# Modulation sums over partitions, moved from matmuls on TensorE to all-reduces on GpSimd

## The chip, the core and the metric

The kernel runs on one core of a Trainium2 chip. The metric is the device time of one execution in microseconds (us), the median of several. The core's engines are named as the profile names them: PE (TensorE), DVE (VectorE), ACT (ScalarE), POOL (GpSimd) and SP (SyncE, which only issues DMAs here).

## The reference, cut

One transformer block over x (1 x 2048 x 512) with adaptive layer norms: six modulation vectors of 512 numbers come from c and w_mod, and shift, scale and gate the two halves of the block.

```python
mod = (_silu(c) @ w_mod).reshape(c.shape[0], 6, 1, -1)
sa, ca, ga, sb, cb, gb = (mod[:, 0], mod[:, 1], mod[:, 2], mod[:, 3], mod[:, 4], mod[:, 5])
h = _layernorm(x, axis=-1) * (1 + ca) + sa
x = x + ga * _A_ref(h, A_wqkv, A_wo)              # linear attention, 32 heads of 16
h = _layernorm(x, axis=-1) * (1 + cb) + sb
x = x + gb * _B_ref(h, B_w_gate, B_w_up, B_w_down)  # (h w_gate * h w_up) w_down
```

All is float32.

## The kernel before, in words

x has 16 tiles of 128 tokens by 512, in 4 chunks of 4. Each float32 operand of a large product is split into a high part (an fp32r rounding, by ACT) and a low part (the difference, by DVE), and a product is three matmuls: high by high, high by low, low by high. Each engine works its own queue in the order in which the code issues it (the schedule is manual: no planner moves anything), and waits on semaphores where it uses what another engine made. Tiles of 128x512 come from one pool of 99 buffers, taken in turn, so a new tile may also wait for the last reader of the buffer's old one.

The first stage makes the modulation vectors sa and ca (v=0 and 1) and K of the first chunk. Then comes the **T loop** (L646 to L695): in step i it issues the K projection of tile i+2 (`proj`, 12 matmuls of 128x512, lines L219 to L221; past the last tile a Q projection), the split of the normalized tile i+1 (`k_split_x`: xh on ACT, xl on DVE at L207) and of phi(K) of tile i+1 (`k_split`: kh on ACT at L363, kl on DVE at L364), in the first two steps of a chunk two transposed columns of the next chunk's norm and their modulation (`modulated`: f on ACT, the high part h as a cast on DVE at L304, the low part at L307), phi of tile i+2 (`k_phi`: two activations, then DVE at L331), the sum z of phi (`z_add`, L357), and `t_tile(i)`, 12 matmuls into four PSUM banks (L372 to L374). In the step before the last, zacc is split, and in the last step two matmuls with a matrix of ones (`over_rows`, L195) sum it over the partitions: zps, from which ACT makes zb. Behind the loop den0 (L706) and the tiles tt (L782 to L787) are made from zb on DVE and ACT, and PE multiplies them (L795).

Into steps 4 to 15 the table `extra` puts work for later, at the end of each step. Part of it are the other four modulation vectors, v = 2 (ga), 3 (sb), 4 (cb) and 5 (gb). For each, `mod_load` issues four DMAs of 128x512 from w_mod, and `mod_part` adds up, on DVE, the four tiles times the four columns of silu(c), into one tile acc of 128x512 (L178 for k=0, L180 for k=1 to 3). What is left is the sum of acc over its 128 partitions. For ga and gb, which are needed as a row repeated on every partition, acc is split (one ACT and one DVE instruction) and `mod_row` multiplies a matrix of ones by both parts on PE (L195) and copies the result from PSUM by ACT (L201). For sb and cb, which are needed as columns (128x4), `mod_col` multiplies each quarter of acc by a vector of ones (L185, a float32 matmul of two passes), and `col_out` adds 0 or 1 on DVE (L190). All four are used only behind the loop: ga at L770, cb and sb at L925, gb at L1280. wo's loads and splits stand in the same table.

Of the kernel before, what the change touches and what calls it, by code (L numbers as in the profile page):

```python
# [7 lines left out]

F32 = mybir.dt.float32
# [1 line left out]
AF = mybir.ActivationFunctionType  # L11
ALU = mybir.AluOpType
AX = mybir.AxisListType

P = 128
# [7 lines left out]
def tile_adaln_block(  # L23
# [12 lines left out]
    nc = tc.nc  # L36
# [3 lines left out]
    KD = D // P  # L40
# [12 lines left out]
    wo_v = wo.rearrange("(k p) n -> k p n", p=P)  # L53
# [20 lines left out]
    def B(tag, shape=(P, D), dt=F32):  # L74

        return T(tiles, tag, shape, dt)
# [32 lines left out]
    def load(src, tag, by=None):  # L109
        raw = B(tag, (P, *src.shape[1:]))[:src.shape[0]]  # L110
        (by or nc.sync).dma_start(raw, src)
        return raw
# [27 lines left out]
    raw_v = load_qkv(2)  # L140
# [38 lines left out]
            else:  # L179
                nc.vector.scalar_tensor_tensor(acc, raws[k], sc[:, k:k + 1], acc, op0=ALU.mult, op1=ALU.add)  # L180

    def mod_col(acc, ps):

        for b in range(KD):
            nc.tensor.matmul(ps[:, b:b + 1], acc[:, b * P:(b + 1) * P], ones, start=True, stop=True)  # L185
        return ps

    def col_out(v, ps, add):
        t = consts.tile([P, KD], F32, name=f"col{v}")
        nc.vector.tensor_scalar(t, ps[:, :KD], add, None, op0=ALU.add)  # L190
        return t

    def over_rows(ps, pair):
        for m, x in enumerate(pair):
            nc.tensor.matmul(ps, ones_r, x, start=m == 0, stop=m == 1)  # L195

    def mod_row(v, pair):
        ps = bank()
        over_rows(ps, pair)
        t = consts.tile([P, D], F32, name=f"row{v}")  # L200
        nc.scalar.activation(t, ps, AF.Copy)  # L201
        return t


# [110 lines left out]
    wk, wq, wv = [], [], []  # L315
# [262 lines left out]
    def mod_load(*vs):  # L578
        raw_m.update({v: load_mod(v) for v in vs})

    def mod_part(v, *ks):
        if 0 in ks:
            accs[v] = B("f")
        mod_acc(accs[v], raw_m[v], ks)

    extra = {4: lambda: (wv.extend(split_raw(r) for r in raw_v[0:1]),),
             5: lambda: (wv.extend(split_raw(r) for r in raw_v[1:2]),),
             6: lambda: (wv.extend(split_raw(r) for r in raw_v[2:3]), mod_load(2),),
             7: lambda: (wv.extend(split_raw(r) for r in raw_v[3:4]),),
             8: lambda: (mod_part(2, 0, 1), mod_load(3)),  # L590
             9: lambda: (mod_part(2, 2, 3), mod_load(4)),
             10: lambda: (accs.update({2: split_raw(accs[2])}), mod_part(3, 0, 1, 2), mod_load(5)),
             11: lambda: (mod_part(3, 3), mod_part(4, 0, 1), rows.update({2: mod_row(2, accs[2])})),
             12: lambda: (raw_o.extend(load(wo_v[k], "raw") for k in range(KD)), mod_part(4, 2, 3), mod_part(5, 0), cols.update({3: col_out(3, mod_col(accs[3], bank()), 0.0)})),
             13: lambda: (mod_part(5, 1, 2, 3), wo_s.extend(split_raw(x) for x in raw_o[:1]), accs.update({5: split_raw(accs[5])}), cols.update({4: col_out(4, mod_col(accs[4], bank()), 1.0)})),
             14: lambda: (wo_s.extend(split_raw(x) for x in raw_o[1:]),), 15: lambda: rows.update({5: mod_row(5, accs[5])})}
    q_at = {4: 3}
    ahead = {}

# [1004 lines left out]
```

## Time and profile before

| | us |
|---|---|
| runs before | 553.54, 553.78, 557.78 (median 553.78) |
| profiled execution, first to last instruction | 552.4 |
| T loop, proj(6) to t_tile(15) on PE | 52.3 to 127.0 |
| PE busy | 545.8 |
| DVE busy | 432.2 |
| ACT busy | 299.5 |
| POOL busy | 176.8 |

The profiled execution's own time is told only as its span, from the first to the last instruction; the runs' times also hold what lies around it, so the median of the runs is 1.4 us above the span. In rows of the timeline the first number is the start in us from the span's start, the second the time until the end, then engine, line, operation, output and inputs, shape and count; in brackets the idle time of the engine before it and what ended that. Matmul rows overlap: the time from one start to the next is what a matmul costs PE (0.23 us for 128x512), the duration is what it takes to come through.

### The profile page before, as it was taken

How to read it: one execution, taken by the hardware profiler on the slowest of the kernel's cores; microseconds unless marked ns; L12 is line 12 of the kernel's file. 1: busy time of each engine (PE TensorE's matmuls, PEld its weight loads, DVE VectorE, ACT ScalarE, POOL GpSimd, SP SyncE). 2: the span in 40 equal slices, each digit the busy share in tenths (PEclk: the TensorE clock that was granted, in tenths of full speed). 3: DMA queues.
4: the chain of work that ended last, by engine and by line, in shares of the span. 5: the costliest groups of instructions: out<-in, count | busy, mean ns of one | idle time of the engine just before them, and what ended most of it. 6: DMA issues, size and time to landing. Idle time of an engine off the chain costs nothing. (4 is left out here: it accounts for less than half of the span.)

```text
span 552.4 us, 8146 instructions
## 1 busy us (share of the span) xinstructions
PE 545.8 (99%) x2775; PEld 460.1 (83%) x2775; DVE 432.2 (78%) x794; ACT 299.5 (54%) x535; POOL 176.8 (32%) x180
## 2 busy tenths in 40 slices
PE   8999999999999999999999999999999999999997
PEld 6888888888888888888888888878888888888886
DVE  6878779978998998865655767797577877879696
ACT  4876857456467876654545355463243534453540
POOL 2000000003527646353556644540002524242400
PEclk9999999999999999999999999999999999999999
DMA  8910224203230045195888634289786534342004
GB/s 256 373 57 1 76 77 152 77 0 77 78 115 2 0 154 189 39 316 180 285 286 274 222 123 163 87 312 391 231 259 218 173 131 138 129 146 86 1 0 153
DMA packets 58512, 83.24 MB, mean 151 GB/s; under 512 B 6564, under 2 KB 23720, under 8 KB 58472
## 3 DMA queue, kind: packets, MB, share of 16 engines
q1 hardware_dynamic: 56544, 81.16, 44.1%
q10 hardware_dynamic: 1928, 1.58, 0.9%
q8 instruction: 22, 0.36, 0.3%
q14 instruction: 18, 0.15, 0.1%
HBM read 53.02 MB, written 29.69 MB: 150 GB/s over the span
## 5 line engine op out<-in xcount | busy, mean ns | idle before, releaser
L1057 PE MATMUL bank<-h,w 128*128 128x512 f32 (+1 forms) x924 | 221.6, 391 | 0.2 <-POOL w L1020 0.2
L1057 PEld LDWEIGHTS bank<-h,w 128*128 128x128 f32 (+1 forms) x924 | 168.2, 186 | 36.2 <-POOL w L1020 0.6
L1063 ACT ACTIVATE bank<-bank 128x512 f32<-128x512 f32 (+2 forms) x46 | 26.2, 571 | 122.7 <-PE bank L1057 122.5
L1253 DVE TENSOR_TENSOR x<-acc,x 128x256 f32<-128x256 f32 x132 | 48.0, 414 | 13.7 <-PE acc L1226 13.1
L1226 PE MATMUL acc<-w,kh 128*128 128x256 f32 x308 | 57.1, 282 | 0.0
L1226 PEld LDWEIGHTS acc<-w,kh 128*128 128x128 f32 x308 | 50.6, 190 | 3.7
L1020 POOL TENSOR_TENSOR w<-raw,w 128x256 fp32r<-128x256 f32 (+3 forms) x22 | 24.7, 1121 | 73.7 <-ACT w L1013 64.1
L219 PE MATMUL bank<-w,h 128*128 128x512 f32 x112 | 44.1, 394 | 0.0
L221 PE MATMUL bank<-w,h 128*128 128x512 f32 x112 | 43.7, 390 | 0.0
L220 PE MATMUL bank<-w,h 128*128 128x512 f32 x112 | 43.6, 390 | 0.0
L1226 PE MATMUL acc<-w,kl 128*128 128x256 f32 x154 | 43.5, 283 | 0.0
L871 PE MATMUL acc<-w,xh 128*128 128x512 f32 x128 | 40.7, 399 | 0.0
L712 POOL TENSOR_TENSOR f<-h,zb 128x512 f32<-128x512 f32 x12 | 17.5, 1468 | 62.9 <-ACT zb L692 48.9
L262 POOL TENSOR_TENSOR rstd<-ve,half 128x4 f32<-128x4 f32 (+3 forms) x12 | 11.2, 935 | 81.4 <-DVE ve L259 68.0
L1083 DVE TENSOR_TENSOR phi<-bank,g 128x512 f32<-128x512 f32 (+1 forms) x22 | 15.1, 687 | 25.2 <-PE bank L1057 25.2
L1063 ACT ACTIVATE u<-bank 128x512 f32<-128x512 f32 (+1 forms) x44 | 26.1, 594 | 15.4 <-PE bank L1057 15.2
L1113 DVE TENSOR_TENSOR g<-bank,u 128x512 f32<-128x512 f32 (+1 forms) x22 | 15.2, 689 | 21.2 <-ACT u L1063 19.9
L1020 POOL TENSOR_TENSOR w<-t,w 128x512 fp32r<-128x512 f32 (+1 forms) x22 | 29.6, 1346 | 0.0
L1146 PE MATMUL acc<-w,kh 128*128 128x512 f32 (+1 forms) x76 | 29.6, 390 | 0.0
L1147 PE MATMUL acc<-w,kh 128*128 128x512 f32 (+1 forms) x76 | 29.6, 390 | 0.0
L1148 PE MATMUL acc<-w,kl 128*128 128x512 f32 (+1 forms) x76 | 29.6, 389 | 0.0
L277 ACT ACTIVATE n<-x,nmr,rstd 128x512 f32<-128x512 f32 x31 | 23.6, 808 | 10.9 <-DVE nmr L267 10.7
(204 smaller groups left out, 1187.0 us busy)
## 6 DMA issues: line engine op xcount, KB each, us to landing
right<-w SPq DMA_DIRECT2D x56, 256.0 KB, 3.7
w<-right SPq DMA_DIRECT2D x56, 256.0 KB, 4.3
x<-in_A_x_dram SPq DMA_DIRECT2D x22, 256.0 KB, 5.2
raw<-in_w_mod_dram SPq DMA_DIRECT2D x22, 256.0 KB, 3.7
raw<-in_B_w_down_dram SPq DMA_DIRECT2D x18, 256.0 KB, 3.0
side_s<-h SPq DMA_DIRECT2D x16, 256.0 KB, 2.6
h<-side_s SPq DMA_DIRECT2D x16, 256.0 KB, 5.3
raw<-in_A_wqkv_dram SPq DMA_DIRECT2D x12, 256.0 KB, 6.2
```

The lines of the kernel that those rows point to most:

```text
L219: nc.tensor.matmul(ps, ah, bh, start=begin and i == 0, stop=False)
L220: nc.tensor.matmul(ps, ah, bl, start=False, stop=False)
L221: nc.tensor.matmul(ps, al, bh, start=False, stop=end and i == n - 1)
L871: nc.tensor.matmul(yps[i], x, y, start=fresh and k + n == 0, stop=k == KD - 1 and n == 2, skip_group_check=True)
L1020: sub = lambda out, x, y: (on or nc.gpsimd).tensor_tensor(out, x, f32(y), op=ALU.subtract)
L1057: mm = lambda x, y, **kw: nc.tensor.matmul(ps, x[:, k], y, skip_group_check=True, **kw)
L1063: nc.scalar.activation(out, x, AF.Copy)
L1146: nc.tensor.matmul(dn[j], hh[:n, a:b], dh[:n], start=i == 0, stop=False)
L1147: nc.tensor.matmul(dn[j], hh[:n, a:b], dl[:n], start=False, stop=False)
L1148: nc.tensor.matmul(dn[j], hl[:n, a:b], dh[:n], start=False, stop=i == n_of - 1)
L1226: mm = lambda x, y, **kw: nc.tensor.matmul(ps, x[:, a:b], y, skip_group_check=True, **kw)
L1253: nc.vector.tensor_tensor(xt[:, halves[at]], banks[b][m], xt[:, halves[at]], op=ALU.add)
```

## The change

The four sums over partitions are made by POOL: `partition_all_reduce` of acc, 128x512, whose result stands on every partition. For the rows that is the result. For the columns the reduced tile is multiplied by the identity, repeated four times (`col_diag`, on POOL), and DVE reduces each 128-wide group to one number (`col_out`: a reduction to 128x4, and for v=4 an addition of 1). The splits of acc, the matmuls, the PSUM banks and the evictions go. The loads of the four vectors move from steps 6, 8, 9 and 10 to steps 4 to 7, the sums on DVE from steps 8 to 13 to steps 6 to 11. The reductions are issued in steps 8 (row 2), 9 (column 3), 10 (column 4) and 11 (row 5, and both multiplications by the identity), `col_out` in steps 13 and 15.

```diff
+    def over_partitions(out, acc):
+        nc.gpsimd.partition_all_reduce(out, acc, channels=P, reduce_op=ReduceOp.add)
+
+    def col_total(v, acc):
+        diag[v] = B("f")
+        over_partitions(diag[v], acc)
+
+    def col_diag(v):
+        t = diag[v].rearrange("p (b i) -> p b i", i=P)
+        nc.gpsimd.tensor_tensor(t, t, ident.unsqueeze(1).to_broadcast([P, KD, P]), op=ALU.mult)
+
+    def col_out(v, add):
         t = consts.tile([P, KD], F32, name=f"col{v}")
-        nc.vector.tensor_scalar(t, ps[:, :KD], add, None, op0=ALU.add)
-        return t
+        nc.vector.reduce_sum(t, diag.pop(v).rearrange("p (b i) -> p b i", i=P), axis=AX.X)
+        if add:
+            nc.vector.tensor_scalar(t, t, add, None, op0=ALU.add)
+        cols[v] = t
...
-    def mod_row(v, pair):
-        ps = bank()
-        over_rows(ps, pair)
+    def mod_row(v, acc):
         t = consts.tile([P, D], F32, name=f"row{v}")
-        nc.scalar.activation(t, ps, AF.Copy)
+        over_partitions(t, acc)
         return t
...
-             6: lambda: (wv.extend(split_raw(r) for r in raw_v[2:3]), mod_load(2),),
-             7: lambda: (wv.extend(split_raw(r) for r in raw_v[3:4]),),
-             8: lambda: (mod_part(2, 0, 1), mod_load(3)),
-             9: lambda: (mod_part(2, 2, 3), mod_load(4)),
-             10: lambda: (accs.update({2: split_raw(accs[2])}), mod_part(3, 0, 1, 2), mod_load(5)),
-             11: lambda: (mod_part(3, 3), mod_part(4, 0, 1), rows.update({2: mod_row(2, accs[2])})),
-             12: lambda: (raw_o.extend(load(wo_v[k], "raw") for k in range(KD)), mod_part(4, 2, 3), mod_part(5, 0), cols.update({3: col_out(3, mod_col(accs[3], bank()), 0.0)})),
-             13: lambda: (mod_part(5, 1, 2, 3), wo_s.extend(split_raw(x) for x in raw_o[:1]), accs.update({5: split_raw(accs[5])}), cols.update({4: col_out(4, mod_col(accs[4], bank()), 1.0)})),
-             14: lambda: (wo_s.extend(split_raw(x) for x in raw_o[1:]),), 15: lambda: rows.update({5: mod_row(5, accs[5])})}
+             4: lambda: (wv.extend(split_raw(r) for r in raw_v[0:1]), mod_load(2)),
+             5: lambda: (wv.extend(split_raw(r) for r in raw_v[1:2]), mod_load(3)),
+             6: lambda: (wv.extend(split_raw(r) for r in raw_v[2:3]), mod_part(2, 0, 1), mod_load(4)),
+             7: lambda: (wv.extend(split_raw(r) for r in raw_v[3:4]), mod_part(2, 2, 3), mod_load(5)),
+             8: lambda: (rows.update({2: mod_row(2, accs[2])}), mod_part(3, 0, 1, 2)),
+             9: lambda: (mod_part(3, 3), mod_part(4, 0, 1), col_total(3, accs.pop(3))),
+             10: lambda: (mod_part(4, 2, 3), mod_part(5, 0), col_total(4, accs.pop(4))),
+             11: lambda: (mod_part(5, 1, 2, 3), rows.update({5: mod_row(5, accs[5])}), col_diag(3), col_diag(4)),
+             12: lambda: (raw_o.extend(load(wo_v[k], "raw") for k in range(KD)),),
+             13: lambda: (wo_s.extend(split_raw(x) for x in raw_o[:1]), col_out(3, 0.0)),
+             14: lambda: (wo_s.extend(split_raw(x) for x in raw_o[1:]),), 15: lambda: col_out(4, 1.0)}
```

In the three places below, names carry a running number that differs between the two programs, and line numbers of the changed kernel are 7 or 8 higher.

POOL's queue from the last norm of the T loop (rstd) to the first product behind the loop (L712 before, L720 now); what stands in brackets are the engines and DMA queues that a row waits for. Before:

```order
L262 TENSOR_TENSOR rstd_885<-ve_887,half 128x4 [waits DVE_49,Activation_49,Pool_49]
L712 TENSOR_TENSOR f_1422<-h_1347,zb 128x512 [waits DVE_49,Activation_49]
L712 TENSOR_TENSOR f_1424<-h_1393,zb 128x512 [waits DVE_49,PE_49]
```

And now:

```order
L269 TENSOR_TENSOR rstd_901<-ve_903,half 128x4 [waits DVE_49,Activation_49,Pool_49]
L184 ISA
L184 ISA row_1060<-f_933 128x512 [waits DVE_49]
L184 ISA f_1130<-f_1062 128x512 [waits DMAHW7_49,DVE_49,PE_49]
L184 ISA f_1174<-f_1127 128x512 [waits DMAHW6_49,DVE_49,Activation_49]
L184 ISA row_1217<-f_1172 128x512 [waits DVE_49]
L193 ISA
L193 TENSOR_TENSOR f_1130<-f_1130,ident 128x512 [waits Pool_49]
L193 TENSOR_TENSOR f_1174<-f_1174,ident 128x512 [waits Pool_49]
L720 TENSOR_TENSOR f_1405<-h_1332,zb 128x512 [waits DMAHW4_49,DVE_49,Activation_49]
```

Between the two stand the four reductions (row 2, column 3, column 4, row 5) and the two multiplications. The two ISA rows without operands switch POOL's loaded library, to the one that has the reduction and back.

DVE's queue in steps 6 and 7 of the T loop, from the low half of a V weight (w from raw) on; xl and kl are what `t_tile` of the next step uses. Before:

```order
L207 TENSOR_TENSOR w_914<-raw_147,w_913 128x512
L207 TENSOR_TENSOR xl_939<-n_697,xh_938 128x512
L364 SCALAR_TENSOR_TENSOR kl_943<-phi_891,kh_942 128x512
L331 SCALAR_TENSOR_TENSOR phi_948<-bank_925,phi_948 128x512
L357 TENSOR_TENSOR z_176<-z_176,phi_891 128x512
L207 TENSOR_TENSOR w_968<-raw_149,w_967 128x512
L207 TENSOR_TENSOR xl_985<-n_699,xh_984 128x512
```

And now:

```order
L214 TENSOR_TENSOR w_930<-raw_147,w_929 128x512
L179 TENSOR_SCALAR f_933<-raw_787,sc 128x512
L181 SCALAR_TENSOR_TENSOR f_933<-raw_789,sc,f_933 128x512
L214 TENSOR_TENSOR xl_958<-n_697,xh_957 128x512
L371 SCALAR_TENSOR_TENSOR kl_962<-phi_907,kh_961 128x512
L338 SCALAR_TENSOR_TENSOR phi_967<-bank_944,phi_967 128x512
L364 TENSOR_TENSOR z_176<-z_176,phi_907 128x512
L214 TENSOR_TENSOR w_987<-raw_149,w_986 128x512
L181 SCALAR_TENSOR_TENSOR f_933<-raw_791,sc,f_933 128x512
L181 SCALAR_TENSOR_TENSOR f_933<-raw_793,sc,f_933 128x512
L214 TENSOR_TENSOR xl_1014<-n_699,xh_1013 128x512
```

The sums of v=2 (f from raw) now stand ahead of xl and kl of step 8, and of xl of step 9.

DVE's queue in step 13 and the start of step 14, now (before, the low half of wo's first tile is followed by that of acc 5, and by an addition of 128x4 from PSUM):

```order
L364 TENSOR_TENSOR z_176<-z_176,phi_1242 128x512 [waits DVE_49]
L214 TENSOR_TENSOR w_1306<-raw_1259,w_1305 128x512 [waits DMAHW5_49,PE_49,Activation_49]
L197 TENSOR_REDUCE col_1309<-f_1130 128x4 [waits Pool_49]
L214 TENSOR_TENSOR xl_1325<-n_972,xh_1324 128x512 [waits Activation_49]
L371 SCALAR_TENSOR_TENSOR kl_1329<-phi_1288,kh_1328 128x512 [waits PE_49,Activation_49]
L338 SCALAR_TENSOR_TENSOR h_1332<-bank_1311,h_1332 128x512 [waits Activation_49]
L364 TENSOR_TENSOR z_176<-z_176,phi_1288 128x512 [waits DVE_49]
```

The reduction to 128x4 (col) waits for POOL's first multiplication, and xl, kl and the last addition to z stand behind it.

More of the change, by code (lines that the diff above doesn't have):

```diff
@@ L6 @@
 from concourse._compat import with_exitstack
+from concourse.bass_isa import ReduceOp
 from concourse.masks import make_identity
@@ L180, in mod_acc @@
                 nc.vector.scalar_tensor_tensor(acc, raws[k], sc[:, k:k + 1], acc, op0=ALU.mult, op1=ALU.add)
[L182 to L188, printed above, removed]
+    def over_partitions(out, acc):
[7 more added lines that the diff above has]
+    def col_out(v, add):
         t = consts.tile([P, KD], F32, name=f"col{v}")
-        nc.vector.tensor_scalar(t, ps[:, :KD], add, None, op0=ALU.add)
-        return t
+        nc.vector.reduce_sum(t, diag.pop(v).rearrange("p (b i) -> p b i", i=P), axis=AX.X)
+        if add:
+            nc.vector.tensor_scalar(t, t, add, None, op0=ALU.add)
+        cols[v] = t
     def over_rows(ps, pair):
@@ L584, in mod_part @@
         mod_acc(accs[v], raw_m[v], ks)
[L586 to L596 removed]
+    diag = {}
+    extra = {4: lambda: (wv.extend(split_raw(r) for r in raw_v[0:1]), mod_load(2)),
+             5: lambda: (wv.extend(split_raw(r) for r in raw_v[1:2]), mod_load(3)),
[8 more added lines that the diff above has]
+             14: lambda: (wo_s.extend(split_raw(x) for x in raw_o[1:]),), 15: lambda: col_out(4, 1.0)}
     q_at = {4: 3}
```

## The prediction

> **What bounds the kernel now.** I read the page's head first, then the waits of TensorE (PE), then the stretches of the T loop.
>
> ```profile
> span 552.4 us, 8146 instructions
> PE 545.8 (99%) x2775; PEld 460.1 (83%) x2775; DVE 432.2 (78%) x794; ACT 299.5 (54%) x535; POOL 176.8 (32%) x180
> core 0: us, PE busy (x) PEld busy (x) DVE busy (x) ACT busy (x) POOL busy (x), PEclk, DMA share, GB/s
> 85.08:91.43 6.35, 6.35 (x33) 5.33 (x32) 6.17 (x12) 4.87 (x9) 0.00 (x0) 1.00 0.42 135
> 91.43:96.90 5.47, 5.47 (x26) 4.53 (x25) 5.37 (x10) 4.18 (x8) 0.00 (x0) 1.00 0.53 181
> ```
>
> PE is busy 99% of the span, at full clock, and in the T loop without a gap: what leaves its queue is won, unless another engine then comes too late. VectorE (DVE) is the one that can: in steps 8 and 9 of the loop (the two stretches) it works 6.17 of 6.35 us and 5.37 of 5.47 us. GpSimd (POOL) does nothing there. The sum goes against the span of 552.4 us; the median of the runs, 553.78 us, is 1.4 us more, which I add at the end.
>
> **What is removed from PE.** The two row sums (pairs of 128x512 matmuls) and the two column sums (eight passes of 128x1 each).
>
> ```profile
> 102.32 0.62 PE L195 MATMUL bank<-w,ones_r 128*128 128x512 f32 x2
> 102.78 0.40 PE L219 MATMUL bank<-w,h 128*128 128x512 f32 x1
> 108.26 0.94 PE L185 MATMUL bank<-ones,f 128*128 128x1 f32 x8
> 109.07 0.49 PE L219 MATMUL bank<-w,h 128*128 128x512 f32 x1
> 109.39 0.40 PE L220 MATMUL bank<-w,h 128*128 128x512 f32 x1
> 114.66 0.95 PE L185 MATMUL bank<-ones,f 128*128 128x1 f32 x8
> 127.00 0.62 PE L195 MATMUL bank<-w,ones_r 128*128 128x512 f32 x2
> 127.46 0.40 PE L219 MATMUL bank<-w,h 128*128 128x512 f32 x1
> ```
>
> From start to start a row pair takes 0.46 us. A column sum takes 0.81 us, and the matmul behind it 0.32 us instead of 0.23, so 0.90 us. Together 2 x 0.46 + 2 x 0.90 = **2.72 us off PE**. ScalarE (ACT) loses two splits and two evictions, DVE two low halves; ACT has room (4.87 of 6.35 us), so that is worth nothing by itself.
>
> **What is moved: modulation sums come two steps sooner on DVE.** The loads stay in their place in SP's queue (the same 16 in the same order, between the x loads and wo); what their buffers wait for lies earlier, and they land long before step 6: nothing. The sums themselves stand in DVE's order ahead of work that PE waits for.
>
> ```profile
> 79.94 0.68 DVE L207 TENSOR_TENSOR xl<-n,xh 128x512 fp32r<-128x512 f32 x1
> 80.55 0.68 DVE L364 SCALAR_TENSOR_TENSOR kl<-phi,kh 128x512 fp32r<-128x512 f32 x1
> 82.32 0.69 DVE L331 SCALAR_TENSOR_TENSOR phi<-bank,phi 128x512 f32<-128x512 f32 x1 [1.09 <-ACT phi L328]
> 88.76 0.48 DVE L178 TENSOR_SCALAR f<-raw,sc 128x512 f32<-128x512 f32 x1
> 89.94 0.68 DVE L207 TENSOR_TENSOR xl<-n,xh 128x512 fp32r<-128x512 f32 x1
> 92.66 0.69 DVE L307 TENSOR_TENSOR h<-f,h 128x512 fp32r<-128x512 f32 x1
> 94.47 1.53 DVE L180 SCALAR_TENSOR_TENSOR f<-raw,sc,f 128x512 f32<-128x512 f32 x2
> 95.92 0.68 DVE L207 TENSOR_TENSOR xl<-n,xh 128x512 fp32r<-128x512 f32 x1
> 98.93 0.48 DVE L178 TENSOR_SCALAR f<-raw,sc 128x512 f32<-128x512 f32 x1
> 100.90 0.69 DVE L207 TENSOR_TENSOR xl<-n,xh 128x512 fp32r<-128x512 f32 x1
> 81.91 0.39 PE L374 MATMUL acc<-kl,xh 128*128 128x512 f32 x1
> 93.93 0.39 PE L221 MATMUL bank<-w,h 128*128 128x512 f32 x1
> ```
>
> A group of sums takes 1.18 us (k=0 and 1: 88.76 to 89.94), 1.45 us (k=2 and 3: 94.47 to 95.92) or 1.97 us (k=0 to 2: 98.93 to 100.90). Step 6 gets 1.18 us, so kl of step 8 starts at 81.73 instead of 80.55 and ends at 82.41; PE wants it at 81.91: 0.5 us late. The idle 1.09 us of DVE before phi (82.32) takes this delay up. Step 7 gets 1.45 us, and step 8 has 1.97 instead of 1.18: DVE is 1.45 + 0.79 = 2.24 us behind (2.27 with what phi keeps) when it makes the low half for the last quarter of proj(12). That ended at 93.35 (92.66 + 0.69) and ends at 95.62; PE wanted it at 93.93. So PE loses 95.62 - 93.93 = **1.7 us** in steps 6 to 9, in which the 0.5 is contained. Bounds: 0.9 us, if ACT and DVE close up by some of their idle time, and 2.5 us, if POOL's reads slow DVE, which the trace shows at another place:
>
> ```profile
> 127.15 0.68 DVE L712 TENSOR_TENSOR f<-h,zb 128x512 f32<-128x512 f32 x1
> 128.47 1.07 DVE L712 TENSOR_TENSOR f<-h,zb 128x512 f32<-128x512 f32 x1
> 125.89 3.10 POOL L712 TENSOR_TENSOR f<-h,zb 128x512 f32<-128x512 f32 x2 [48.86 <-ACT zb L692]
> ```
>
> Beside POOL's tiles one of two equal DVE instructions took 0.39 us more; two such behind the first reduction make the 0.8 us of the upper bound. I take none. Later steps have slack: by step 11 DVE is about 2.0 us behind (through step 10 it has done 1.18 + 1.45 + 1.97 + 1.85 + 1.9 = 8.35 us of sums and splits of sums, instead of 1.18 + 1.45 + 2.57 = 5.2, less the 1.09), and wants nothing of PE before PE, itself 1.7 us later, gets there.
>
> **What is added on POOL**, in order: a library switch, four reductions of 128x512 (row 2, column 3, column 4, row 5), a switch back, two multiplications with the identity. DVE then reduces each product to 128x4; col_out(3) stands in DVE's queue in step 13, ahead of xl, kl and phi of step 14, of zacc's last addition, and so of the row sum zps for which PE waits.
>
> ```profile
> 76.02 1.01 POOL L262 TENSOR_TENSOR rstd<-ve,half 128x4 f32<-128x4 f32 x1 [19.79 <-DVE ve L259]
> 144.60 1.31 POOL L712 TENSOR_TENSOR f<-h,zb 128x512 f32<-128x512 f32 x1 [1.34 <-PE bank L220]
> masks.py:199 POOLq MODIFY_POOL_CONFIG  x2: 11/11/11, 0.9 to 1.0; - x2
> DMA to landing us min/median/max: 2.2/3.1/8.1
> ```
>
> No reduction over partitions is in this trace. Below, every partition must be read before any result is written: two passes of a tile at 1.31 us, 2.6 us. Above, 128 partitions folded in halves are seven passes and the writing an eighth: 10.5 us. A plain single pass would be 1.3 us, and one column at a time, at the pow's 0.23 us per column (0.91 us for 4), 118 us. Nothing in the trace is nearer to one end of 2.6 and 10.5, so I take the middle by ratio, **R = 5.2 us**.
>
> A switch is a pair of MODIFY_POOL_CONFIG. The one pair shown takes 0.02 us, but it calls the library that is there already. Code that is not there must come by DMA, and a transfer lands after 2.2 to 8.1 us, 3.1 at the median. I take two landings, **6.2 us**, between 0 and 8.1. The first switch follows the pow at 76.02, in idle time: nothing. The Trainium skill (GPSIMD Engine Reference, section 2.1, Instruction dispatch) gives the first call to a newly loaded kernel about 6 us of loading that no profile row shows; by the trace's 0.02 us the sum would be the first rival's, by the page's 6 us nearly my forecast, and no run here shows which.
>
> Now the chain. Column 3's reduction takes a buffer that t_tile(10)'s last matmul frees, and row 5's sums are complete in step 11:
>
> ```profile
> 96.65 0.39 PE L374 MATMUL acc<-kl,xh 128*128 128x512 f32 x1
> 103.31 0.75 DVE L180 SCALAR_TENSOR_TENSOR f<-raw,sc,f 128x512 f32<-128x512 f32 x1
> 113.43 0.69 DVE L331 SCALAR_TENSOR_TENSOR phi<-bank,phi 128x512 f32<-128x512 f32 x1 [1.99 <-ACT phi L328]
> 119.93 0.69 DVE L331 SCALAR_TENSOR_TENSOR h<-bank,h 128x512 f32<-128x512 f32 x1 [0.31 <-ACT h L328]
> ```
>
> Column 3 starts at 97.0 + 1.7 = 98.7. Row 5's sums end at 103.31 + 2.0 + 2.2 = 107.6 us, but POOL is then still at column 4, until 98.7 + 2R = 109.1. The first product is ready at 109.1 + 5.2 + 6.2 + 1.5 = **122.0 us**. DVE reaches col_out(3) at about 115.6 (phi at 113.43, with PE 0.33 late there, then the additions of two more tiles), and can wait: h at 119.93 waits for ACT and PE anyway, now at 119.2. Before it stand col_out, xl and kl, 0.6 us each: a product at 117.4 us costs nothing. zps had 1.4 us of slack behind that (122.6 to 124.0), though DVE's backlog eats some of it ahead of den0 and tt. I let PE stall from 118.1 us on, the middle of 117.4 and 118.8. The stall is 122.0 - 118.1 = **3.9 us**. Its bounds: 0 and, for 10.5 us a reduction, 19.8.
>
> Shorter waits come first only for larger R: xh of step 10 on ACT takes the buffer of row 2's input (free at 85.7 + R, wanted at 92.3), xl of step 13 that of column 3's (98.7 + R, wanted at 110).
>
> Behind the loop col_out(4) puts 0.7 us of DVE ahead of den0 and tt, which feed PE at 133 us with about 0.4 us to spare: **0.3 us**. Sum: -2.72 + 1.7 + 3.9 + 0.3 = +3.2 us. The span becomes 555.6 us, the median **557.0 us**.
>
> **Rivals.**
> 1. *POOL is in time.* R below about 3.5, or a cheap switch with R below 6. For it: POOL has idle time from 77 to 125 us. Against it: four reductions are one chain with a switch in it. PE keeps -2.72 + 1.7 + 0.3 = -0.7: 553.1 us. Chance 0.27.
> 2. *POOL's reductions queue up.* At 10.5 us each they follow one another from 98.7 us without a gap; the product comes at 98.7 + 31.5 + 7.7 = 137.9, DVE stands at col_out(3), and PE stalls 19.8 us: 572.9 us. Each us more of R costs three. This decides from R = 6.0, where the loss passes 1%. For it: POOL needs 1.3 us even for an addition of tiles. Chance 0.28.
> 3. *A column at a time*, as the pow's row: 98.7 + 354 + 7.7 puts the product at 460 us: a stall of 342 us, 895 us. Chance 0.03. The skill (same page, section 3.2, Cross-partition) gives a partition-axis reduction of 128x2048 247.7 us; a quarter, an estimate of 62 us, would give about 728 us. That this instruction works so, no run here shows.
> 4. *DVE keeps up and POOL too*: all of 2.72 us stays, 551.1 us. Against it stand the two full stretches. Chance 0.04.
>
> **How the numbers follow.** The forecast, a product some us late, has 0.38; its own range is 553.8 us (R = 3.5) to 559.3 (R = 6.0). About 1% can be told from no change here, 548.2 to 559.3 us. Slower by more: 0.28 + 0.03 and a tail of 0.03 of the forecast's, 0.34. Faster: PE's whole removal is 0.5%, so only what I do not see, 0.02. Within 1%: 0.64. The range reaches down past rival 1 with PE's smaller loss (553.1 - 0.8, less some noise: 551.5) and up into rival 2 (R = 9.9: 571).
>
> **What would show it.** In the profile after: no rows for column and row sums on PE; PE idle near 82 and 93 us, waiting for DVE's kl and the low halves of h, 1.7 us in all; a gap of DVE before the reduction to 128x4, ended by POOL's product, about 6 us long; a gap of about 6 us on POOL between the last reduction and the first product; a PE wait for zacc's halves near 123 us. I am wrong if PE has no wait in steps 7 to 9, if the product is ready before DVE asks for it, or if reductions take over 6 us and stand end to end.

## The result, and the profile after

The changed kernel takes 563.6 us (median of 5 runs, 562.76 to 564.95), the kernel before 554.2 us beside it: a ratio of 1.0169, 95% interval 1.0147 to 1.0191. It is 1.7% slower, where "within 1%" was forecast. The head of its page:

```profile
span 561.6 us, 8121 instructions
PE 548.8 (98%) x2755; PEld 459.6 (82%) x2755; DVE 440.8 (78%) x793; ACT 296.9 (53%) x531; POOL 192.6 (34%) x186
```

PE has 20 matmuls less and yet 3.0 us more busy time; DVE has one instruction less and 8.6 us more busy time. So instructions that were there before take longer. The waits of PE (the line that waited, who was waited for, us in total, times, longest):

```profile
PE bank L226 <- DVE h L311: 2.5, 1, 2.5
...
PE bank L204 <- ACT w L213: 2.0, 1, 2.0
...
PE acc L803 <- ACT w L792: 0.5, 1, 0.5
PE acc L803 <- DVE w L795: 0.4, 1, 0.4
...
PE acc L381 <- DVE kl L371: 0.2, 1, 0.2
```

The first is the last quarter of proj(12), the second the row sum zps at the end of the T loop, the next two the kv products behind the loop (L803, the products of the tiles tt). The places were named in the prediction; the sizes forecast there were others (1.7, 3.9 and 0.3 us). The timeline of POOL:

```profile
85.80 3.58 POOL L184 PARTITION_ALL_REDUCE row<-f  x1 [8.81 <-DVE f L181]
100.11 3.32 POOL L184 PARTITION_ALL_REDUCE f<-f  x1 [10.74 <-DVE f L181]
107.00 3.33 POOL L184 PARTITION_ALL_REDUCE f<-f  x1 [3.57 <-ACT phi L335]
114.02 3.61 POOL L184 PARTITION_ALL_REDUCE row<-f  x1 [3.69 <-DVE f L181]
124.27 2.55 POOL L193 TENSOR_TENSOR f<-f,ident 128x512 f32<-128x512 f32 x2 [6.64 <-issue]
```

A reduction takes 3.3 to 3.6 us. Between two of them POOL waits for other engines, for DVE's sums in all but one case, so they do not queue up. Between the last and the first product lie 6.64 us in which POOL waits for nothing that the profile shows: the library switch. The timeline of DVE at the same times:

```profile
86.18 2.73 DVE L371 SCALAR_TENSOR_TENSOR kl<-phi,kh 128x512 fp32r<-128x512 f32 x1
88.83 0.82 DVE L311 CAST h<-f 128x512 fp32r<-128x512 f32 x1
...
100.38 2.61 DVE L181 SCALAR_TENSOR_TENSOR f<-raw,sc,f 128x512 f32<-128x512 f32 x1
...
107.16 2.73 DVE L214 TENSOR_TENSOR xl<-n,xh 128x512 fp32r<-128x512 f32 x1
...
114.45 2.73 DVE L371 SCALAR_TENSOR_TENSOR kl<-phi,kh 128x512 fp32r<-128x512 f32 x1
...
125.59 0.69 DVE L197 TENSOR_REDUCE col<-f 128x4 f32<-128x512 f32 x1 [3.97 <-POOL f L193]
126.19 1.18 DVE L214 TENSOR_TENSOR xl<-n,xh 128x512 fp32r<-128x512 f32 x1
```

This is what to look for: behind the start of each reduction stands one DVE instruction with two inputs in SBUF that takes 2.61 to 2.73 us, where the same instruction takes 0.68 to 0.75 elsewhere. Four times 1.9 to 2.05 us are 8.0 of the 8.6 us of busy time: DVE does not work longer, it stands. The cast behind the first hold has one input and takes 0.82 instead of 0.42 us, so it was slowed too. The last two rows show the wait for POOL's product (3.97 us), and that the products hold DVE too (1.18 instead of 0.68 us).

PE's own busy time grows for the most part with the granted clock. Three stretches of two us (after the busy times of PE, its weight loads, DVE, ACT and POOL, each with a count, comes PEclk):

```profile
core 0: us, PE busy (x) PEld busy (x) DVE busy (x) ACT busy (x) POOL busy (x), PEclk, DMA share, GB/s
98.00:100.00 2.00, 1.94 (x5) 1.49 (x5) 2.00 (x5) 1.25 (x3) 0.00 (x0) 0.53 0.00 0
102.00:104.00 2.00, 2.00 (x11) 1.62 (x10) 2.00 (x3) 0.00 (x0) 1.44 (x1) 1.00 0.18 18
142.00:144.00 2.00, 2.00 (x14) 2.00 (x13) 1.75 (x3) 1.48 (x3) 0.00 (x0) 0.62 0.87 219
```

Behind the wait at proj(12), and again in the kv products, PE's clock is 0.50 for 3.41 us (98.10 to 101.52 and 142.48 to 145.89 us in the trace's clock record; the 0.53 and 0.62 above are means of stretches that begin earlier): five matmuls in two us instead of eleven.

Where the time went is read by comparing the start of one and the same matmul in two traces. Three serve in all that follows: A is the last matmul of proj(12) (93.93 us before), B the first behind the place of row 5's sum (127.46 us before), C one in the y steps (199.92 us before). All four removed sums lie between A and B. A reads the steps with the full DVE, B the whole loop with 2.72 us of removal in it, C what comes behind the loop. In the changed kernel A is 4.21 us later, B 6.33, C 9.18, and so it stays to the end.

### The profile page after: what moved, and what is told of

It reads as the page before. It is cut to its first block, busy times and chain, and to the rows that moved or that the text cites. A ratio compares the mean times of both kernels' runs of the same rounds, so it can differ in the third digit from the quotient of the medians.

```text
span 561.6 us, 8121 instructions
## 1 busy us (share of the span) xinstructions
PE 548.8 (98%) x2755; PEld 459.6 (82%) x2755; DVE 440.8 (78%) x793; ACT 296.9 (53%) x531; POOL 192.6 (34%) x186
## 5 line engine op out<-in xcount | busy, mean ns | idle before, releaser
L226 PE MATMUL bank<-w,h 128*128 128x512 f32 x112 | 44.6, 398 | 2.5 <-DVE h L311 2.5
L228 PE MATMUL bank<-w,h 128*128 128x512 f32 x112 | 44.4, 396 | 0.1
L227 PE MATMUL bank<-w,h 128*128 128x512 f32 x112 | 44.0, 392 | 0.0
L1234 PEld LDWEIGHTS acc<-w,kl 128*128 128x128 f32 x154 | 29.4, 191 | 0.0
```

What stands on the lines that cost most here:

```text
L226: nc.tensor.matmul(ps, ah, bh, start=begin and i == 0, stop=False)
L227: nc.tensor.matmul(ps, ah, bl, start=False, stop=False)
L228: nc.tensor.matmul(ps, al, bh, start=False, stop=end and i == n - 1)
L1234: mm = lambda x, y, **kw: nc.tensor.matmul(ps, x[:, a:b], y, skip_group_check=True, **kw)
```

## The experiments

The theory, H in the expectations: a reduction on POOL holds a two-operand DVE instruction for 2.05 us, and where DVE has no time to spare PE pays for it. The rivals: M, the sums moved two steps sooner make the loss; C, the wait for POOL's chain makes it. What all runs gave, with the starts of A, B and C against the kernel before:

```
run              us       before   ratio   95% interval      A      B      C
changed kernel   563.6    554.2    1.0169  1.0147 to 1.0191  +4.21  +6.33  +9.18
e1_sooner        556.83   554.45   1.0039  1.0025 to 1.0053  +1.80  +1.94  +1.92
e2_no_reduction  557.42   554.45   1.0054  1.0038 to 1.0070  +3.84  +1.11  +1.86
e3_columns_late  558.86   554.45   1.0076  1.0062 to 1.0090  +4.76  +3.68  +4.24
e4_old_steps     560.55   554.45   1.0118  1.0093 to 1.0143  +0.19  +4.14  +5.39
e5_full_step     556.2    554.21   1.0038  1.0025 to 1.0051  +2.01  +2.14  +2.13
e6_next_step     554.25   554.21   1.0010  0.9991 to 1.0030  -0.02  -0.01  -0.03
e7_halves        560.76   554.21   1.0122  1.0108 to 1.0136  +3.53  +6.83  +6.75
e8_two_late      553.54   554.21   0.9993  0.9984 to 1.0002  -0.05  -0.78  -0.66
e9_dve_product   559.99   553.77   1.0095  1.0068 to 1.0121  +4.61  +3.97  +6.76
e10_act_terms    553.03   553.77   0.9983  0.9960 to 1.0006  +0.07  -1.39  -1.39
e11_no_hold      555.24   553.85   1.0025  1.0014 to 1.0037  +1.84  -0.91  +0.84
```

**The move alone (e1).** The kernel before, with the table of the loads and sums as in the change, and the sums over partitions on PE in their old steps:

```diff
-             8: lambda: (mod_part(2, 0, 1), mod_load(3)),
-             9: lambda: (mod_part(2, 2, 3), mod_load(4)),
...
+             6: lambda: (wv.extend(split_raw(r) for r in raw_v[2:3]), mod_part(2, 0, 1), mod_load(4)),
+             7: lambda: (wv.extend(split_raw(r) for r in raw_v[3:4]), mod_part(2, 2, 3), mod_load(5)),
...
```

> The kernel before, with the modulation loads and their weighted sums two steps sooner as in the change, but the sums over partitions still on PE, in their old steps. Theory H (each reduction on GpSimd holds a two-operand VectorE instruction for 2.05 us, and in the full steps PE pays for it): nothing holds VectorE here, so the move costs only its own 1.7 us of PE wait in steps 6 to 9, with at most 1.5 us of lower granted clock behind it: +1.7 us against the kernel before (0.9 to 3.2). Theory M (the move itself makes the loss, because VectorE is full in steps 7 to 9): +6 us or more, with PE waits of 4 us by proj(12). Theory C (the wait of the first column for GpSimd's chain makes it): +1.7 us or less.

Measured: +2.4 us. A comes 1.80 us later and B 1.94, so the loss falls where it was forecast, and nothing follows. M falls as the cause of 9 us. The list of waits shows little of it:

```profile
PE bank L219 <- DVE h L304: 0.2, 1, 0.2
```

The rest of the 1.8 us lies in steps too short for that list: behind this wait six matmuls of proj(12) start 0.33 to 0.46 us apart instead of 0.23. DVE's casts and low halves end at 93.81, 94.54, 94.88 and 95.67 us, and matmuls start at 93.87, 94.60, 94.93 and 95.73.

**No reductions (e2).** The changed kernel, with the four reductions replaced:

```diff
-        nc.gpsimd.partition_all_reduce(out, acc, channels=P, reduce_op=ReduceOp.add)
+        nc.gpsimd.memset(out, 0.0)
```

> The changed kernel with each of the four reductions over partitions replaced by one GpSimd memset of its output: it leaves out the sums over partitions of these four vectors, and so the library switch; the products with the identity, the sums over the free axis and their places stay. Theory H: no hold, no switch, so PE keeps 2.72 us less 1.7 us for the move and about 0.3 us behind the loop: -0.7 us against the kernel before (-1.5 to +1.0 if the clock dips). VectorE's two-operand instructions in steps 8 to 12 take 0.7 us, none 2.6 us. Theory M: nothing changes in steps 6 to 9, so the loss stays at +5 us or more. Theory C: -0.7 us, as by H.

Measured: +3.0 us, a miss: H had said -0.7, at most +1.0. PE's wait at proj(12) is nearly that of the changed kernel, with no reduction there:

```profile
PE bank L226 <- DVE h L311: 2.4, 1, 2.4
```

The timeline of POOL in this run, and below it that of DVE, tell why:

```profile
85.93 0.53 POOL L184 MEMSET f<- 128x512 f32 x1 [8.48 <-PE acc L381]
...
91.54 3.50 POOL L193 TENSOR_TENSOR f<-f,ident 128x512 f32<-128x512 f32 x2
```

```profile
86.15 0.69 DVE L371 SCALAR_TENSOR_TENSOR kl<-phi,kh 128x512 fp32r<-128x512 f32 x1
...
92.12 1.79 DVE L214 TENSOR_TENSOR xl<-n,xh 128x512 fp32r<-128x512 f32 x1
93.84 1.75 DVE L371 SCALAR_TENSOR_TENSOR kl<-phi,kh 128x512 fp32r<-128x512 f32 x1
```

With nothing to wait for, the two products with the identity came 33 us sooner, into the worst place, and held two DVE instructions 1.1 us each. So the experiment had not taken the holds away, it had put others there. It also shows what does not hold: the memset at 85.93, which only writes, leaves kl beside it at 0.69 us. The Trainium skill (SBUF — State Buffer, section Who interferes with whom) has the rule: a VectorE instruction with two SBUF inputs contends with a GpSimd instruction that reads SBUF, and not with one that only writes it. These rows agree. For this case it gives no time; in the changed kernel the hold is 1.9 to 2.05 us beside a reduction whose row is 3.3 to 3.6 us long.

**No reads on POOL in the loop (e11).** So the run was made again, with the products and column sums on DVE behind the loop besides:

```diff
-        nc.gpsimd.partition_all_reduce(out, acc, channels=P, reduce_op=ReduceOp.add)
+        nc.gpsimd.memset(out, 0.0)
...
-        nc.gpsimd.tensor_tensor(t, t, ident.unsqueeze(1).to_broadcast([P, KD, P]), op=ALU.mult)
+        nc.vector.tensor_tensor(t, t, ident.unsqueeze(1).to_broadcast([P, KD, P]), op=ALU.mult)
...
+    col_diag(3)
+    col_diag(4)
+    col_out(3, 0.0)
+    col_out(4, 1.0)
     y_step(1, after=[lambda: den_t(5), lambda: den_q(8)])
```

> The changed kernel with each reduction over partitions replaced by a GpSimd memset of its output (it leaves out the sums over partitions of these four vectors), and with the two products and the column sums on VectorE behind the T loop, ahead of the second y step: now GpSimd reads no tile in the loop at all. In the run with the memsets alone, the two products had moved forward to 91.5 us and held two VectorE instructions 1.1 us each, which theory H did not see coming. Theory H: without them what is left is PE's removal and the move as measured alone: -2.72 + 2.4 = -0.3 us against the kernel before (-1.2 to +0.8), no VectorE instruction of this loop over 0.8 us for one 128x512 tile, and at most 0.3 us of PE wait at proj(12). Rival (something else of the new order, such as the two more f tiles in the ring of buffers, makes the loss of that run): +2 us or more.

Measured: +1.4 us, 0.6 above the bound given. In the loop H is right to the tenth: A is 1.84 us later (the move alone: 1.80), and B is 0.91 us sooner, where -2.72 + 1.9 = -0.8 was due. What was left out of the expectation is the column work at its new place, where PE then waits:

```profile
PE bank L854 <- DVE h L755: 1.5, 2, 1.1
...
PE bank L226 <- DVE h L311: 0.2, 1, 0.2
```

From B to C this run loses 1.75 us, of which these two waits at L854 are 1.5. So without POOL's reads the changed order of the loop is worth its 0.9 us. The rival's +2 us or more did not come.

**One spare reduction, in two places (e5 and e6).** The kernel before with one reduction more whose result is not used, once in the full step 8, once a step later:

```diff
-             8: lambda: (mod_part(2, 0, 1), mod_load(3)),
+             8: lambda: (mod_part(2, 0, 1), dummy(2), mod_load(3)),
```

> The kernel before, with one more reduction over partitions on GpSimd of the half-made sum of row 2, in step 8 (about 90 us), its result unused: nothing is moved or removed, and nothing waits for it. Theory H (the reduction holds a two-operand VectorE instruction 2.05 us): the low half of step 8's tile takes 2.7 us instead of 0.68, VectorE ends the low half for the last quarter of proj(12) at 95.4 us instead of 93.35, where PE wants it at 93.93: a PE wait of about 1.5 us, and with a clock dip up to 3: +1.5 us against the kernel before (1.0 to 3.0). Rival (the reduction costs PE only through those who wait for its result): 0.0 us.

```diff
-             9: lambda: (mod_part(2, 2, 3), mod_load(4)),
+             9: lambda: (mod_part(2, 2, 3), dummy(2), mod_load(4)),
```

> The same kernel with that spare reduction one step later, of the finished sum of row 2, at about 96 us: Theory H: the same instruction, the same hold of 2.05 us (one two-operand VectorE instruction of 2.6 to 2.7 us), but VectorE is not late there and has 0.6 us of idle time at 106 and 2.0 us at 111: 0 to +0.5 us against the kernel before. If a reduction cost PE a fixed amount wherever it stands (its own library switch, memory traffic), the two runs with a spare reduction would be alike.

Measured: +2.0 us in step 8, 0.0 us a step later. The instruction held is of the same kind and length in both. In the first DVE's kl at 90.62 us, in the second its kl at 96.55:

```profile
90.62 2.73 DVE L372 SCALAR_TENSOR_TENSOR kl<-phi,kh 128x512 fp32r<-128x512 f32 x1
```

```profile
96.55 2.73 DVE L372 SCALAR_TENSOR_TENSOR kl<-phi,kh 128x512 fp32r<-128x512 f32 x1
```

In the first run PE waits for it at proj(12), and A is 2.01 us later:

```profile
PE bank L227 <- DVE h L312: 1.2, 1, 1.2
```

In the second A, B and C stay within 0.03 us of the kernel before. Nothing waits for the spare result, so the rival of e5 (a reduction costs only through those who wait for it) falls, and so does a fixed price per reduction. The hold is the same in both; what it costs is set by DVE's slack at that place.

**Halves (e7).** The changed kernel with each reduction as two of 128x256:

```diff
-        nc.gpsimd.partition_all_reduce(out, acc, channels=P, reduce_op=ReduceOp.add)
+        for h in range(2):
+            c = slice(h * D // 2, (h + 1) * D // 2)
+            nc.gpsimd.partition_all_reduce(out[:, c], acc[:, c], channels=P, reduce_op=ReduceOp.add)
```

> The changed kernel with each reduction over partitions as two of 128x256. If the hold goes with what is read (theory H, as for a shared way to memory), each half holds VectorE about 1.0 us, VectorE's total stays about 8 us above that of the kernel before, and the time stays within 2 us of the changed kernel: +8 to +12 us against the kernel before. If the hold is a fixed cost of the instruction, eight holds of 2.05 us make VectorE's total 16 us larger, and the time grows to +14 us or more.

Measured: +6.6 us, below the range of either, 2.8 us better than the changed kernel. The two rows of DVE beside row 2's halves:

```profile
86.15 1.58 DVE L373 SCALAR_TENSOR_TENSOR kl<-phi,kh 128x512 fp32r<-128x512 f32 x1
...
88.29 1.39 DVE L316 TENSOR_TENSOR h<-f,h 128x512 fp32r<-128x512 f32 x1
```

These halves hold 0.9 and 0.7 us, the other six 0.3 to 0.9, all eight 5.9 us where four whole reductions hold 8.0: the hold is no fixed cost of the instruction. DVE can work between the halves, and its busy time falls from 440.8 to 438.6 us. In the loop that is won at first and lost again: the matmul behind column 4's place (115.46 us before) is 1.40 us late instead of 4.17, but then PE waits 3.8 us for zps instead of 2.0, and B is later than in the changed kernel. The 2.8 us of the time come from behind the loop, where this run has no listed wait in the kv products and no low clock.

**Columns late (e3).** The changed kernel with the two column outputs behind the loop:

```diff
-             13: lambda: (wo_s.extend(split_raw(x) for x in raw_o[:1]), col_out(3, 0.0)),
-             14: lambda: (wo_s.extend(split_raw(x) for x in raw_o[1:]),), 15: lambda: col_out(4, 1.0)}
+             13: lambda: (wo_s.extend(split_raw(x) for x in raw_o[:1]),),
+             14: lambda: (wo_s.extend(split_raw(x) for x in raw_o[1:]),)}
...
+    col_out(3, 0.0)
+    col_out(4, 1.0)
     y_step(1, after=[lambda: den_t(5), lambda: den_q(8)])
```

> The changed kernel with the two column outputs (VectorE's reduction of the products to 128x4 and the addition) taken out of the T loop and put behind it, ahead of the second y step; reductions and products stay where they are. It takes away the wait of VectorE for GpSimd's chain, not the holds. Theory H: steps 7 to 12 stay as in the changed kernel (PE there 6.9 us later less 2.7 us); only the 2.8 us of wait before zps and the 0.9 to 2.4 us before kv go: +4 to +6 us against the kernel before, with four VectorE instructions of 2.6 to 2.7 us. Theory M: the same +4 to +6 us, but told apart from H by the first two runs. Theory C: all of the loss goes, -1 to 0 us.

Measured: +4.4 us, within H's range. The wait at zps is gone; that at proj(12) stands, with one for kl that the hold at 114 us makes:

```profile
PE bank L226 <- DVE h L311: 2.5, 1, 2.5
...
PE acc L381 <- DVE kl L371: 1.0, 1, 1.0
```

C falls as the whole cause, and stands for half of it: with the column outputs late, 9.4 - 4.4 = 5.0 us go, each run taken against the kernel before beside it. B, 3.68 us later with the removal and the move in it, prices the four holds: 3.68 + 2.72 - 1.94 = 4.5 us of PE, of 8.0 us of DVE. Against e11, which has the same removal and move and no reads on POOL in the loop, it is 3.68 + 0.91 = 4.6.

**The products on DVE (e9).** The changed kernel with the products right ahead of the column reductions, on DVE:

```diff
-        nc.gpsimd.tensor_tensor(t, t, ident.unsqueeze(1).to_broadcast([P, KD, P]), op=ALU.mult)
+        nc.vector.tensor_tensor(t, t, ident.unsqueeze(1).to_broadcast([P, KD, P]), op=ALU.mult)
...
-             13: lambda: (wo_s.extend(split_raw(x) for x in raw_o[:1]), col_out(3, 0.0)),
+             13: lambda: (wo_s.extend(split_raw(x) for x in raw_o[:1]), col_diag(3), col_out(3, 0.0)),
```

> The changed kernel with the two products with the identity on VectorE, right ahead of its two column reductions, in steps 13 and 15, instead of on GpSimd: GpSimd makes only the four reductions there, and VectorE waits for no library switch. If the wait ahead of the row sum zps is the switch (6.64 us between the last reduction and the first product in the changed kernel), it goes: column 3's total is ready at 103.4 us, ten us before VectorE asks for it, and VectorE has only 1.2 us more for each column. Then the time is that of the run with late column outputs (+4.7 us against the kernel before) and up to 1.2 us: +4.5 to +6 us, with no VectorE wait for GpSimd in the loop. If it is the reductions that come too late, the wait stays and so does the time: +8 us or more.

Measured: +6.2 us, just above the upper end. DVE waits for POOL no more, and B is at +3.97, as with late columns (+3.68): the wait ahead of zps was for POOL's product. That the switch made it, and not row 5's reduction ahead of the product, follows from the rows of the changed kernel: that reduction ends at 117.6 us, so that without the 6.64 us the first product would be ready at 118.9, and DVE asks at 121.6. But from B to C this run loses 2.8 us, as the changed kernel does (9.18 - 6.33 = 2.85). What both have there is the output of column 4 in DVE's queue, ahead of what kv needs:

```profile
130.31 0.68 DVE L193 TENSOR_TENSOR f<-f,ident 128x512 f32<-128x512 f32 x1
131.03 0.69 DVE L197 TENSOR_REDUCE col<-f 128x4 f32<-128x512 f32 x1
131.75 0.42 DVE L199 TENSOR_SCALAR col<-col 128x4 f32<-128x4 f32 x1
132.09 0.67 DVE L714 TENSOR_REDUCE den<-zb 128x32 f32<-128x512 f32 x1
```

In the changed kernel PE's listed waits in kv are 0.46 and 0.40 us, and the rest of the 2.85 falls in the stretch of low clock that begins at 142.48 us. The run without reductions (e2) tells the two apart: it has column 4's output at the same place, a wait of 0.40 us in kv and no low clock, and loses 0.75 us from B to C. So about 2 us go with the low clock, which this run has too, from 140.15 us on; half of 3.41 us is 1.7.

**The old steps (e4).** The run with late columns, with the loads and sums in their old steps, and the reductions in steps 10 to 13:

```diff
-             8: lambda: (rows.update({2: mod_row(2, accs[2])}), mod_part(3, 0, 1, 2)),
+             8: lambda: (mod_part(2, 0, 1), mod_load(3)),
+             10: lambda: (rows.update({2: mod_row(2, accs[2])}), mod_part(3, 0, 1, 2), mod_load(5)),
...
```

> The run with late column outputs, and besides with the modulation loads and weighted sums in the steps of the kernel before: reductions of row 2, column 3, column 4 and row 5 in steps 10, 11, 12 and 13. It keeps the holds and takes away the move. Theory H: PE keeps 2.72 us, and the four holds of 2.05 us fall in steps in which VectorE has some more room, so part of the 8.2 us reaches PE: -1 to +4 us against the kernel before, with four VectorE instructions of 2.6 to 2.7 us and a PE wait for VectorE behind some of them. Theory M: -2.7 us, no PE wait for VectorE. Theory C: -2.7 us.

Measured: +6.1 us, worse than any theory had it. Up to the place of column 4's sum all goes as hoped: the matmul behind it starts 2.07 us sooner than before (115.46 us there). Then comes one long wait, at zps:

```profile
PE bank L204 <- ACT w L213: 3.8, 1, 3.8
```

DVE had no idle time left from 97 to 124 us, and each hold moved its last addition to z, from which zps is made. The three rows are the hold at 120 us, that addition, and the low half behind it:

```profile
120.23 2.73 DVE L214 TENSOR_TENSOR xl<-n,xh 128x512 fp32r<-128x512 f32 x1
...
124.09 0.68 DVE L364 TENSOR_TENSOR z<-z,phi 128x512 f32<-128x512 f32 x1
125.47 0.69 DVE L214 TENSOR_TENSOR w<-z,w 128x512 fp32r<-128x512 f32 x1 [0.69 <-ACT w L213]
```

Before, z's last addition starts at 120.54 us. Four holds, 8.0 us, less 2.9 us of idle time that DVE had up to there, less 1.4 us of low halves and column evictions that went, make 3.7 us; it is 3.55. Behind the wait PE's clock was 0.50 until 131.2 us, for 5.7 us, of which half is lost. The wait of 3.8 and this 2.9, less the 0.46 us of row 5's matmuls, make the step from 2.07 us sooner to 4.14 us later.

**Only what fits (e8).** From that account a version follows: two reductions in the two places with room, the column by DMA to memory and back, column 4 and row 5 on PE as before:

```diff
-             10: lambda: (accs.update({2: split_raw(accs[2])}), mod_part(3, 0, 1, 2), mod_load(5)),
-             11: lambda: (mod_part(3, 3), mod_part(4, 0, 1), rows.update({2: mod_row(2, accs[2])})),
+             10: lambda: (rows.update({2: row_total(2, accs[2])}), mod_part(3, 0, 1, 2), mod_load(5)),
+             11: lambda: (mod_part(3, 3), mod_part(4, 0, 1), cols.update({3: col_total(3, accs[3])})),
...
+    def col_by_dma(v):
+        flat.append(tc.dram_tile([1, D], F32, name=f"flat{v}"))
+        nc.sync.dma_start(flat[0], cols.pop(v)[0:1])
+
+    def col_back(v):
+        t = consts.tile([P, KD], F32, name=f"col{v}")
+        nc.sync.dma_start(t, flat[0].rearrange("o (k p) -> p (o k)", p=P))
```

> A version that should beat both: the kernel before, in its own steps, with row 2's reduction in step 10 and column 3's in step 11 on GpSimd (the two places where the run with the old steps showed no PE loss); the column comes out of the reduced row by a DMA to memory and back, so that no product and no VectorE reduction is needed; column 4 and row 5 stay on PE. PE loses 0.46 + 0.90 = 1.36 us of work. By theory H the two holds make 4.1 us of VectorE, less 2.9 us of its idle time up to 120 us and 0.9 us of work taken away: zacc's last addition is 0.4 us later, PE 1.4 us sooner with 1.2 us of slack: about 0.6 us of new wait ahead of the row sum zps: -0.8 us against the kernel before (-1.4 to +0.5). If holds cost PE their full 4.1 us anywhere: +2.7 us.

Then the same, with the first terms of three sums on ACT (e10):

```diff
-        mod_acc(accs[v], raw_m[v], ks)
+        mod_acc(accs[v], raw_m[v], ks, nc.scalar if v > 2 else None)
```

> The version with row 2 and column 3 on GpSimd in steps 10 and 11, and the first term of the weighted sums of modulations 3, 4 and 5 (three of 128x512 at 0.48 us) on ScalarE instead of VectorE. By theory H what is left of the two holds at zps is 0.6 us of PE; VectorE is relieved of 1.4 us ahead of it, so all of 1.36 us should stay: -1.4 us against the kernel before (-1.8 to -0.6), 0.6 us below the version without it, and z's last addition at about 120.0 us instead of 121.0. If something else than VectorE's backlog takes the 0.6 us, nothing changes: -0.7 us.

Measured: -0.7 us in either, each beside its own runs of the kernel before. z's last addition on DVE, in the first and in the second:

```profile
121.00 0.68 DVE L380 TENSOR_TENSOR z<-z,phi 128x512 f32<-128x512 f32 x1
```

```profile
119.31 0.68 DVE L380 TENSOR_TENSOR z<-z,phi 128x512 f32<-128x512 f32 x1
```

The first is 0.46 us later than before, as worked out (0.4), and B keeps 0.78 of 1.36 us. In the second z is 1.2 us sooner than before, and B and C keep 1.39 us: all of it. That z comes 0.7 us sooner than the 120.0 worked out is in part luck with the place. Here column 3's reduction has a longer row than any other, and its hold falls on an earlier addition to z and is 1.45 us, not 1.9:

```profile
105.31 4.76 POOL L184 PARTITION_ALL_REDUCE f<-f  x1 [5.45 <-PE bank L244]
107.50 2.13 DVE L380 TENSOR_TENSOR z<-z,phi 128x512 f32<-128x512 f32 x1
```

So the account holds in the traces, but for this. In the times it can not be told from no change: both intervals reach 1, and the second run's time is the -0.7 us of its rival. Both beat the changed kernel; that either beats the kernel before is not shown.

## Why the prediction was wrong, point by point

The parts of the loss at C, from the runs:

```
term                           forecast   measured   from
sums taken off PE              -2.72      -2.7       B in e10 (-1.39 of 1.36), A and B in e11
sums two steps sooner          +1.7       +1.9       e1
POOL's reads hold DVE          0          +4.5       B in e3
wait at zps for the product    +3.9       +2.65      B, changed kernel against e3
behind the loop                +0.3       +2.85      B to C, changed kernel
sum                            +3.2       +9.2
```

- **PE is the bound, and what is removed**: right, to 0.03 us where nothing else touches it.
- **The move**: right in place and size: 1.7 forecast, 1.9 measured, with kl of step 8 late by 0.57 (0.5 forecast).
- **"Beside POOL's tiles one of two equal DVE instructions took 0.39 us more; two such behind the first reduction make the 0.8 us of the upper bound. I take none."** This is the step that failed. The mechanism stood there, and its row too; its size was taken from one overlap, as a bound, and only for the first of four reductions. The kernel before has longer holds later in its trace, such as this one of 1.15 us (0.68 us without):

```profile
461.60 1.83 DVE L1083 TENSOR_TENSOR phi<-g,g 128x512 f32<-128x512 f32 x1
461.58 1.29 POOL L1218 TENSOR_TENSOR w<-t,w 128x512 fp32r<-128x512 f32 x1
```

A reduction of 128x512 holds 1.9 to 2.05 us, four times, and this costs PE 4.5 us in the loop, where the forecast had 0. In the full steps this adds to the move without anything to soften it: 1.8 us (e1) and 2.0 us (e5) make 3.8 apart, and 4.2 to 4.8 together at A (the changed kernel, e3), since each had used the same slack of PE of 0.6 us.
- **The reductions**: 5.2 us forecast, 3.3 to 3.6 measured; the 62 us of the third rival is far off. **The switch**: 6.2 forecast, 6.64 measured (7.1 in e3 and e7), so the Trainium skill's 6 us (GPSIMD Engine Reference, section 2.1, Instruction dispatch) agrees with this trace.
- **The chain**: the first product was forecast for 122.0 us and came at about 125.6 us, though the reductions were faster. Row 5's reduction started at 114.02 us instead of 109.1, since DVE, held three times, had the sums late. PE was later by then as well, so that the wait at zps cost 2.65 us and not 3.9.
- **Behind the loop**: right that column 4's output makes kv late, wrong in size: 0.86 us of waits, and with the low clock behind them 2.85. The sum had no term for a lower clock.
- **The rivals**: with R at 3.3 to 3.6 the first rival's condition was all but met, and its time of 553.1 us was still 10 us off, since it left the holds out as the forecast did. The second did not come: POOL stood idle 3.6 us between reductions. The third and the fourth did not come either.
- **Two slips in the numbers**: at R = 3.5 the chain puts the product at 116.9 us, ahead of the 117.4 that costs nothing, so the lower end of the forecast's own range is 553.1 and not 553.8 us. The row shown for the pow has 1.01 us for 4 columns, not 0.91. Neither moves the forecast.

The time lay inside the range only because its upper part stood for slow reductions, and they were fast: that is luck. The change itself, +9.4 us, is three times the +3.2 forecast.

What stays open: when the clock falls. The holds and waits were taken away one by one; the clock was only seen to follow them. Behind the loop it goes with about 2 us (e2 against the changed kernel and e9). The stretch behind proj(12) shows no loss at B: e3 has it and stands at +3.68, e9 has not and stands at +3.97. All these starts come from one trace of each kernel, and are no surer than some tenths of a us: the changed kernel, e3 and e9 have the same edits up to A, and their A is at +4.21, +4.76 and +4.61.

## What to carry to other kernels

Before work goes to GpSimd because it is idle, look at VectorE at the same place: a GpSimd instruction that reads SBUF can stop a VectorE instruction with two SBUF inputs, so a full VectorE pays for an idle GpSimd. Price such a move by VectorE's idle time up to the next point where the bounding engine waits for it, and sum the holds up to there: that account gave B of e8 and e10 to 0.1 us (not z of e10), where four holds at once did not fit. An experiment that takes an operation away moves what stood behind it: look where that lands before you read the time.

## What the runs showed of the hardware

- A reduction over partitions of 128x512 takes 3.3 to 3.6 us on GpSimd and holds a VectorE instruction with two SBUF inputs 1.9 to 2.05 us (once, in e10, 4.76 and 1.45); one of 128x256 holds 0.3 to 0.9, a product of 128x512 with the identity up to 1.1 us. A memset holds nothing, and DVE's reduction to 128x4 (0.69 us beside the products) was not held either.
- VectorE is not always the one that waits. In e9 its product at 130.31 us began 0.03 us ahead of two GpSimd products (L720) and took its 0.68 us; those two took 3.07 us together, in the changed kernel 2.55.
- A short wait of PE can cost more than itself. With a wait of 3.8 us the granted clock fell to 0.50 in both runs that had one (e4, e7). With one of about 2.5 us (2.47) it fell so in the changed kernel and in e3, and did not in e9 (2.45 us) and e2 (2.38 us); after 2.0 us it did not fall (the changed kernel, e7). It stayed low for 3.41 us, in e4 for twice that. The Trainium skill (TensorE: Matmul & The Clock Gate, section What's actually happening) puts the half clock after an idle window of some 3.4 us that runs freely, so that the moment varies. That waits of one length end differently agrees, and so do the 3.41 us; but waits of 2.5 us were enough here, and in kv even 0.9 us in all.
